# Attention and long convolution in one kernel: a filter reversal placed later, a later last transpose, more blocks for VectorE near the end, four extra matmuls

## The chip, the cores and the metric

The kernel runs on one core of a Trainium2 chip. The metric is the device time in microseconds (us) of one execution. Executions of the kernel before took 864.25, 865.54, 867.79 and 869.4 us; their median is 866.66 us.

The core has a matrix engine (TensorE, PE in the profile; PEld are its weight loads), a vector engine (VectorE, DVE), a scalar engine (ScalarE, ACT), GpSimd (POOL) and SyncE (SP). Here POOL and SP mostly issue transfers. Matrix products land in PSUM[...].

## The reference: two halves side by side

With S = 2048 positions and D = 512 channels, the left half of the output is multi-head attention with 32 heads of 16 channels:

```
qkv = x @ wqkv;  p = softmax(q k^T * 16**-0.5);  left = (p v) @ wo
```

The right half is a gated long convolution, written with FFTs in the reference:

```
k_shift = causal 4-tap convolution of k with shift_k
kv      = k_shift * v
y       = causal convolution of kv with ssm_k (2048 taps per channel) + kv * ssm_D
right   = q * y
```

## The kernel before: blocks, steps and two planned orders

**Attention.** Scores are made in blocks of 128 keys x 512 queries for one head. There are 2048 such blocks: 4 query blocks x 8 groups of 4 heads x 16 key tiles x 4 heads. They are handled in 741 steps, numbered by `T`. In a step TensorE writes two or three blocks into two or three PSUM banks (`emit_qk`, line 536), and ScalarE turns them into exponentials with one instruction (`PT`, line 547). Even and odd steps use different banks (0 to 2 and 3 to 5). Two steps later TensorE multiplies the exponentials by the values (`pv_step`, `emit_pv`, line 629). When all blocks of a group of heads are in, VectorE transposes, divides and transposes back (`finish_group`, lines 693 to 715), and the output projection uses the result (`op_mm`, line 746).

The number of blocks of a step is fixed in `banks_of`: 2 in odd steps below 184 and in 75 steps that leave a bank to other work, 2 as soon as at most `2 * N_TAIL` blocks are left, else 3. With `N_TAIL = 9` the last eight steps (733 to 740) have two blocks each.

**Exponentials on VectorE.** In some steps of three blocks, VectorE takes the exponential of the third block in five passes of 128 x 512 (`exp_on_dve`, lines 583, 590 three times, 595). `dve_block` decides in which. It refuses steps below 56 and from `NT - N_TAIL - GAP` = 741 - 9 - 7 = 725 on, and it refuses when the planned work of VectorE is too far ahead (`BACKLOG`). In the trace 212 blocks are made so, the last in step 724.

**Convolution.** The filter is reversed along its length, padded and stored to a scratch tensor in DRAM, so that each channel's Toeplitz matrix can be read with one transfer of overlapping rows. VectorE makes the reversal: four copies of 128 x 2048 (`kz_turn`, line 423) that wait for `h_kzl`, the last of three loads on one semaphore (two of the filter, one of `ssm_D`), then `kz_store` (line 428) adds `ssm_D` and issues the store. `kz_turn` also issues, after its second copy, the transposed load of the first half of k (`load_kt(0)`), and `kz_store` issues that of the second half; both go to the SP queue, and a small POOL memset goes with each. All later Toeplitz loads (512 of 512 KB, line 784 by way of 220) are on the SP queue too, and wait for the store.

The convolution itself is 128 quads of four channels (`conv_lags`, line 801, bank `BGB` = 7). After eight quads, `conv_turn` (line 827) transposes the sums, which VectorE has copied from PSUM into `YB` (line 816), and VectorE multiplies them by q into `QN` (line 836). The last `conv_turn` is issued from `emit_bg` itself, and when nothing is left for bank 7, `emit_bg` issues `keep_busy` (line 1012), a matmul whose result nobody reads, once a step until step 731. Others of that kind are made by `warm_up` (line 1007) where a gap is planned. From step 732 on, `tail_mm` makes the first three quarters of the projections of the last query block.

**What sets the order.** A planner in the kernel's code writes each engine's instruction list before the program is built. Each engine has a planned clock (`pe.t`, `dve.t`) and each instruction a planned duration. VectorE's work that isn't urgent lies in lists (`flow`); `pick` takes the entry that can start earliest and whose `gate()` is true, and `urgent` and `advance` let such entries in before the next urgent instruction. On the chip each engine runs its list in that order, and waits on semaphores.

At the very end, outside the loop, `op_mm(qb, 3, 0, 3, ...)` makes the first three quarters of the fourth projection tile, and then each of four tiles gets its last quarter as soon as its part of the last transposed group (`OTN`) is there; VectorE and ScalarE copy the results out in turn (`op_out_end`, lines 764 and 766), and four transfers store them.

## Time and profile before

| what | before |
|---|---|
| median of 4 executions | 866.66 us |
| the profiled execution, its own time | 865.5 us |
| its span in the profile | 863.8 us |
| ScalarE busy | 838.1 us, 97% |
| VectorE busy | 780.3 us, 90% |
| TensorE busy | 741.7 us, 86% |
| first exponential starts | 9.35 us |
| last exponential ends | 856.2 us |
| steps, blocks on VectorE | 741, 212 |

The span runs from the first to the last instruction that the profiler saw. An engine's row gives its busy time; the rest of the span it waited or had nothing to do. "Idle before" a row is that engine's wait just ahead of it, and the name behind the arrow is what ended the wait. PEclk is the share of its clock that TensorE was granted. In the list by time, a row with x3 merges three instructions in a row.

### The profile page before, as it was taken

To read this page: it belongs to the slowest core of one execution; us is meant where nothing else is said; L and a number is where in the kernel's file an instruction comes from. 1 tells how busy PE (TensorE), PEld (TensorE's weight loads), DVE (VectorE), ACT (ScalarE), POOL (GpSimd) and SP (SyncE) were. 2 spreads that over 40 slices of the span, in tenths; PEclk is the share of its full clock that TensorE was granted. 3 is DMA by queue.
4 is the path that set the end of the run, shared out by engine and by line. 5 is a ranking of instruction groups with operands and counts; after the bars stand their busy time and mean duration, and the time that the engine had idled before them with its cause. 6 is when DMAs were issued, how large, how long until landed. Compare 5 with 4: busy or idle time off the path is not lost.

```text
span 863.8 us, 29370 instructions
## 1 busy us (share of the span) xinstructions
PE 741.7 (86%) x13142; PEld 302.9 (35%) x13180; DVE 780.3 (90%) x1325; ACT 838.1 (97%) x746; POOL 17.4 (2%) x33
## 2 busy tenths in 40 slices
PE   7888999998888888888888888888888889888877
PEld 2223343443333333333333333334333333333332
DVE  3228899999999999999999999999999999999992
ACT  6999999999999999999999999999999999999996
POOL 2000000000000000000000010000000000000000
PEclk9999899999999999999999999999999999999998
DMA  9960069779999999999999999999999999999941
GB/s 270 267 225 1 1 194 338 249 257 319 407 408 408 385 395 395 405 407 404 380 397 380 359 407 391 387 363 379 407 409 378 377 399 410 408 406 407 408 157 57
DMA packets 104813, 289.36 MB, mean 335 GB/s; under 512 B 35184, under 2 KB 37232, under 8 KB 104304
## 3 DMA queue, kind: packets, MB, share of 16 engines
q1 hardware_dynamic: 99424, 279.35, 85.8%
q0 software_dynamic: 1808, 6.29, 2.1%
q8 instruction: 104, 1.70, 0.8%
q10 hardware_dynamic: 3456, 1.84, 0.8%
q14 instruction: 21, 0.17, 0.0%
HBM read 276.83 MB, written 6.42 MB: 328 GB/s over the span
## 4 chain that ended last, share of the span: by engine, by line
ACT 53%; DVE 20%; DMA 13%; PE 9%; SPq 2%; issue 2%; ACTq 0%
ACT PT L547 53%; DMA WR<-kz_scratch 12%; DVE EH L590 9%; PE PS L536 3%; DVE FX L583 3%; DVE PTD L595 3%; SPq L220 2%; PE PS L629 2%; PE PS L801 2%; DMA WR<-in_B_ssm_D_dram 1%; DVE QT L377 1%; DVE DT L693 1%; DVE YB L816 1%; PE PS L746 0%; DVE QN L836 0%
## 5 line engine op out<-in xcount | busy, mean ns | idle before, releaser
L547 ACT ACTIVATE PT<-PS 128x1536 bf16<-128x1536 f32 (+1 forms) x741 | 835.1, 1345 | 12.5 <-PE PS L536 11.3
L536 PE MATMUL PS<-QT,KTo 32*128 32x512 bf16 x2048 | 304.7, 389 | 86.5 <-ACT PT L547 68.5
L590 DVE SCALAR_TENSOR_TENSOR EH<-EH,FX 128x512 f32<-128x512 f32 x424 | 281.2, 679 | 0.1
L801 PE MATMUL PS<-WR,KV 128*5 128x128 bf16 (+15 forms) x8192 | 223.3, 221 | 13.5 <-DMA WR<-kz_scratch 11.5
L629 PE MATMUL PS<-PT,VAF 128*32 128x512 bf16 x1836 | 202.7, 394 | 5.0 <-DVE DT L693 3.4
L801 PEld LDWEIGHTS PS<-WR,KV 128*2 128x2 bf16 (+15 forms) x8192 | 149.2, 88 | 99.2 <-issue 40.0
L536 PEld LDWEIGHTS PS<-QT,KTo 32*128 32x128 bf16 x2048 | 73.0, 91 | 264.3 <-ACT PT L547 225.5
L583 DVE TENSOR_SCALAR FX<-PS 128x512 f32<-128x512 f32 x212 | 144.8, 683 | 7.5 <-PE PS L536 7.1
L595 DVE SCALAR_TENSOR_TENSOR PTD<-EH,FX 128x512 uint16<-128x512 f32 x212 | 143.2, 677 | 0.3 <-PE PS L629 0.3
L590 DVE SCALAR_TENSOR_TENSOR EH<-FX 128x512 f32<-128x512 uint16 x212 | 142.8, 682 | 0.0
L629 PEld LDWEIGHTS PS<-PT,VAF 128*32 128x32 bf16 x1836 | 48.6, 93 | 120.8 <-issue 106.2
L1007 PE MATMUL PS<-IDN,ZW 128*32 128x512 bf16 (+3 forms) x228 | 72.2, 317 | 0.3 <-PE PS L629 0.3
L629 PE MATMUL PS<-PTD,VAF 128*32 128x512 bf16 x212 | 60.8, 388 | 0.0
L693 DVE STREAM_TRANSPOSE DT<-PS 128x512 f32<-128x512 f32 x31 | 22.1, 712 | 16.9 <-PE PS L629 16.5
L402 DVE CAST VAF<-PS 128x512 bf16<-128x512 f32 x16 | 11.1, 691 | 27.9 <-PE PS L360 27.9
L1007 PEld LDWEIGHTS PS<-IDN,ZW 128*32 128x32 bf16 x228 | 22.0, 96 | 11.6 <-issue 10.3
L377 DVE TENSOR_SCALAR QT<-PS,MASK 128x512 bf16<-128x512 f32 x30 | 21.0, 742 | 3.0 <-PE PS L332 2.8
L816 DVE CAST YB<-PS 128x512 bf16<-128x512 f32 x32 | 21.8, 681 | 1.1 <-PE PS L801 0.9
L360 PE MATMUL PS<-WKV,xT 128*128 128x512 bf16 x59 | 17.7, 383 | 3.7 <-DVE VAF L402 2.6
L746 PE MATMUL PS<-WKV,OTN 128*128 128x512 bf16 x53 | 18.6, 411 | 2.2 <-issue 1.0
L341 PE MATMUL PS<-xT,WKV 128*128 128x512 bf16 (+1 forms) x57 | 16.7, 376 | 2.0 <-issue 1.0
L382 DVE CAST KTo<-PS 128x512 bf16<-128x512 f32 (+1 forms) x16 | 10.7, 670 | 7.7 <-PE PS L341 7.6
(64 smaller groups left out, 202.6 us busy)
## 6 DMA issues: line engine op xcount, KB each, us to landing
WR<-kz_scratch SPq DMA_DIRECT2D x512, 512.0 KB, 8.0
kz_scratch<-WR SPq DMA_DIRECT2D x1, 2176.0 KB, 8.6
QN<-in_B_q_dram POOLq DMA_DIRECT2D x2, 1024.0 KB, 12.4
out_dram<-QN POOLq DMA_DIRECT2D x2, 1024.0 KB, 8.2
out_dram<-OUTA POOLq DMA_DIRECT2D x12, 128.0 KB, 5.4
QN<-in_B_ssm_k_dram SPq DMA_DIRECT2D x1, 1024.0 KB, 5.9
QT<-in_B_ssm_k_dram SPq DMA_DIRECT2D x1, 1024.0 KB, 7.9
WR<-in_B_v_dram SPq DMA_DIRECT2D x2, 512.0 KB, 7.0
```

Source lines behind the costliest of these rows:

```text
L377: lambda e, par=par: e.tensor_scalar(QT[:, qb % 2, 2 * o + par, :], PS[:, bank, :], MASK[:, par:par + 1], None, ALU.mult),
L536: ins = e.matmul(PS[:, bank, :], lhsT=KTo[32 * s:32 * s + 32, g // 2, kt * 128:(kt + 1) * 128], rhs=QT[32 * s:32 * s + 32, qb % 2, g, :], ...
L547: h_exp[T] = act.op(lambda e: e.activation(PT[:, T % R_PT, 0:n * QB], PS[:, banks[0]:banks[0] + n, :].rearrange("p b f -> p (b f)"), ACT.E ...
L583: h_f = urgent(lambda e: e.tensor_scalar(fx, PS[:, bank, :], FIX_ADD, FIX_HI, ALU.add, ALU.min), [h, h_last.get(i - R_FX)], slack=0.6)
L590: st["h"] = dve.op(lambda e: e.scalar_tensor_tensor(eh, src, (A3, A2, A1)[j], frac, ALU.add, ALU.mult), [st["h"], h_last.get(i - R_EH), h_ ...
L595: lambda e: e.scalar_tensor_tensor(out16, eh, A4, fx, ALU.mult, ALU.add),
L629: ins = e.matmul(dst, lhsT=w, rhs=rhs, start=(k == 0), stop=(k == KT - 1), tile_position=(0, 32 * s))
L693: h_t = urgent(lambda e: e.transpose(out=dt, in_=PS[:, pvb(n), :]), [h] + before, slack=0.1, us=(0.63, 0.751))
L746: ins = e.matmul(PS[:, bank, :], lhsT=OTN[:, (4 * qb + o) % R_O, t * 128:(t + 1) * 128], rhs=WO[:, o, :], start=(o == 0), stop=(o == 3))
L801: ins = e.matmul(PS[32 * c:32 * c + NB - n, BGB, 128 * (kk % 4):128 * (kk % 4) + 128], lhsT=KV[:, qd, n:NB, c], rhs=WR[:, r + c, 128 * (NB ...
L816: hh = urgent(lambda e: e.tensor_copy(YB[:, half, :].rearrange("p (k i) -> p k i", k=4), src), [h, h_yb[0]], slack=0.3, us=V512)
L1007: pe.op(lambda e: e.matmul(PS[32 * s:32 * s + 32, pvb(n), 0:128 * k], lhsT=ZW[:, :], rhs=rhs, start=False, stop=False, tile_position=(0, 3 ...
```

## The change

Five constants and four places are touched.

- `N_TAIL` goes from 9 to 7: the steps of two blocks at the end begin at step 734. There are six of them, and the last step (740) has one block. The number of steps stays 741, since 184 + 75 + 475 steps come before.
- `dve_block` uses a new constant `TAIL_GAP = 4` in place of `GAP = 7`: its bound goes from step 725 to 741 - 7 - 4 = 730.
- The four reversals get a gate: the planner lets one in only when VectorE's planned clock is at least 4 us (`KZ_LATE`) past the planned landing of `h_kzl`.
- The last `conv_turn` is put off, step by step, while the planned end of VectorE's copy into `YB` isn't at least 0.2 us before TensorE's planned clock; at the latest it is issued in step 731.
- At the end, `KEEP` = 4 matmuls of 128 x 128 by 128 x 512 are added between the three quarters of the fourth projection tile and the four last quarters. They wait for the last exponential, and write the bank that it read; nobody reads their result.

```diff
-N_TAIL = 9
+N_TAIL = 7
...
 GAP = 7
+TAIL_GAP = 4
 AHEAD = 4
+KZ_LATE = 4.0
+KEEP = 4
...
     for c in (2, 3, 0, 1):
-        piece(lambda us, c=c: kz_turn(c, us), lambda: [h_kzl])
+        piece(lambda us, c=c: kz_turn(c, us), lambda: [h_kzl], gate=lambda: dve.t >= at(h_kzl) + KZ_LATE)
     piece(kz_store, lambda: [h_kzt[0]], (0.1, 0.22))
...
     def dve_block(T):
-        if len(banks_of[T]) < 3 or T < T_DVE or T >= NT - N_TAIL - GAP:
+        if len(banks_of[T]) < 3 or T < T_DVE or T >= NT - N_TAIL - TAIL_GAP:
             return None
...
         if st["turn"] and st["qd"] == C // 4:
+            if T < min(tail_mm) - 1 and at(h_ybw[0]) > pe.t - 0.2:
+                return
             conv_turn(C // 32 - 1, BGB)
...
     op_mm(qb, 3, 0, 3, tail_banks[3])
+    for i in range(KEEP):
+        pe.op(lambda e: e.matmul(PS[:, banks_of[NT - 1][0], :], lhsT=IDN[:, :], rhs=WO[:, 0, :], start=True, stop=True),
+              [h_exp[NT - 1]], inc=i == KEEP - 1)
     for t in range(4):
         h = op_mm(qb, t, 3, 4, tail_banks[t])
```

## Prediction

> **What bounds the kernel now.** I read the busy shares and slices of the page first.

> ```profile
> span 863.8 us, 29370 instructions
> PE 741.7 (86%) x13142; PEld 302.9 (35%) x13180; DVE 780.3 (90%) x1325; ACT 838.1 (97%) x746; POOL 17.4 (2%) x33
> ACT  6999999999999999999999999999999999999996
> ```

> ScalarE works from 9.35 to 856.2 us with hardly a pause, and those 847 us hold 741 exponentials and about 11.3 us of waits of over 0.08 us each (I summed the "idle before" of its rows in order of time). So only three things shorten the kernel: fewer blocks on ScalarE, shorter waits of ScalarE, or a shorter end after 856.2. The groups of instructions, shapes apart, give the price of a block:

> ```profile
> L547 ACT ACTIVATE PT<-PS 128x1536 bf16<-128x1536 f32 x354 | 528.5, 1559 | 8.5 <-PE PS L536 8.0
> L547 ACT ACTIVATE PT<-PS 128x1024 bf16<-128x1024 f32 x387 | 409.7, 1148 | 4.1 <-PE PS L536 3.3
> ```

> 528.5 / 354 = 1.493 and 409.7 / 387 = 1.059: a block is 0.43 us. Then the head, VectorE and SP by time:

> ```profile
> 15.04 0.42 DVE L382 CAST KTo<-PS 128x256 bf16<-128x256 f32 x1 [1.03 <-PE PS L341]
> 17.63 1.30 DVE L423 COPY WR<-QN 128x2048 bf16<-128x2048 bf16 x2 [2.17 <-DMA WR<-in_B_ssm_D_dram]
> 18.84 0.69 DVE L402 CAST VAF<-PS 128x512 bf16<-128x512 f32 x1
> 19.45 1.29 DVE L423 COPY WR<-QT 128x2048 bf16<-128x2048 bf16 x2
> ...
> 27.59 6.12 SPq L220 DMA_TRANSPOSE QN<-in_B_k_dram  x1
> 33.83 0.50 SPq L220 DMA_DIRECT2D kz_scratch<-WR  x1
> ```

> VectorE stood 2.17 us at the reversal before its transfer had landed, and a copy of values queued behind came at 18.84. SP took up the loads that need the reversal only at 27.59. What ScalarE lost there:

> ```profile
> 20.56 1.02 ACT L547 ACTIVATE PT<-PS 128x1024 bf16<-128x1024 f32 x1 [0.56 <-PE PS L536]
> ...
> 23.57 4.66 ACT L547 ACTIVATE PT<-PS 128x1024 bf16<-128x1024 f32 x4 [0.36 <-PE PS L536]
> ```

> Last the end: TensorE and ScalarE by time, and the granted clock in stretches (columns: length, busy time of PE, PEld, DVE, ACT, POOL, then clock, DMA share, GB/s).

> ```profile
> 837.40 0.62 PE L827 MATMUL PS<-IDN,YB 128*128 128x128 bf16 x8 [1.14 <-DVE YB L816]
> 838.39 2.79 ACT L547 ACTIVATE PT<-PS 128x1536 bf16<-128x1536 f32 x2 [0.31 <-PE PS L536]
> 843.40 12.81 ACT L547 ACTIVATE PT<-PS 128x1536 bf16<-128x1536 f32 x12 [0.59 <-PE PS L536]
> 858.79 1.89 PE L746 MATMUL PS<-WKV,OTN 128*128 128x512 bf16 x4 [0.52 <-DVE OTN L715]
> ...
> 835.80:839.20 3.40, 1.74 (x21) 0.92 (x22) 3.29 (x6) 3.09 (x4) 0.16 (x1) 1.00 0.00 0
> 839.20:842.60 3.40, 3.40 (x17) 0.62 (x17) 3.25 (x6) 3.22 (x3) 1.02 (x1) 0.50 0.51 147
> ...
> 852.90:856.30 3.40, 2.41 (x19) 0.68 (x18) 0.00 (x0) 3.32 (x4) 0.00 (x0) 1.00 0.00 0
> 856.30:863.80 7.50, 3.64 (x8) 0.86 (x9) 3.67 (x9) 1.19 (x2) 0.00 (x0) 0.50 0.21 70
> ```

> The last `conv_turn` held TensorE for 1.14 us; the stretch in which that fell has 1.74 us of PE, and the next runs at half clock, in which ScalarE waits 0.18 and 0.59 us more. From 856.3 the clock is half again, for all of the final products.

> [...] the half-clock stretches here last 3.4 us or a multiple, and the two at the end each follow a thin one (1.74 and 2.41 us of PE; stretches with 2.98 and 3.40 were followed by a full clock). [...] the last four products start at 858.79, 859.19, 859.62 and 860.04, so 0.42 us apart. [...]

> **The change part by part**, against the profiled execution (865.5 us, of which 863.8 is the span; the median is 1.2 higher).

> *Reversal later.* No instruction is added. The four copies (1.30 + 1.29 us) go some 4 us later. There VectorE idles 0.47, 1.13, 2.30, 1.13 and 1.26 us ahead of its rows from 21.4 to 30.0 us, and the planner puts single copies of 0.65 us into such gaps. The 2.17 us wait goes, for the load landed at 17.6. ScalarE gets back at most 0.56 + 0.17 (at 21.75) + 0.36 + 0.16 (at 28.38) = 1.25 us; at least nothing, if the copies then hold up other casts. I take 0.8: the 0.56 wholly and part of the rest. What moves with it: two transposed loads and the store on SP, two memsets on POOL. The reversal would end near 24 to 26 us; SP is busy with x and v until 27.59 and takes the store at 33.83, POOL has nothing until 132 us. So it costs nothing with 2 to 8 us of cover; and past it, k is first multiplied at 93.5 us and the first load from the scratch is issued at 44, so some 50 us more. VectorE's order in between is otherwise the same, and a planner that only compares its own clocks with each other, when all of them shift alike, decides the same afterwards. So steps 30 to 724 should keep their order.

> *Last turn later.* TensorE then issues the scores of step 726 and their products first, one step of 1.33 us; the copy to `YB` ended at 837.35, so its wait is nearly over by then. Behind the waiting turn stood the scores of 726, and ScalarE behind those: 0.31 us back. If the stretch then holds enough PE work, the half clock at 839 goes too: 0.18 + 0.59 us. What is late next: `keep_busy` in the following step waits for VectorE's product into `QN` (it waited about 0.4 us before), and the 1024 KB store of `QN` on POOL leaves 1.3 us later, with its 8.2 us hidden under the 25 us to the end. Range 0 to 1.1, taken 0.6.

> *More blocks on VectorE.* ScalarE's blocks fell to two in steps 713, 716, 718, 721 and 724: one VectorE block per 2.6 steps. Five more steps (725 to 729) give 2, at 0.43 us each: 0.85 us back; one to three are 0.4 to 1.3. Their 5 x 0.6 us each lie in VectorE's idle time from 843.5 to 856.9 (13.41 us ahead of the last transpose). The change's own words say "up to step 722", which its code doesn't (730 is the bound); were it so, one block fewer, 0.4 us lost.

> *Tail of two-block steps.* The blocks are the same and so is the number of exponentials, so ScalarE's total stays. After the last exponential one product follows instead of two: 0 to 0.2 us, taken 0.1.

> *Four matmuls at the end.* If the clock is half (as before), the three products start at 856.81 and take 3 x 0.43 to 858.1, the four new ones 1.7 more to 859.8, and the first final product starts there instead of at 858.79: 1.0 us lost. If it is full, all seven (1.5 us) end by 858.4, behind VectorE's 1.5 us of transpose, reciprocal and product, and cost nothing, and the four final ones, 0.22 apart, end about 0.8 us earlier. [...] I take 0.1 lost, with -0.9 and +1.0 as ends.

> Sum: -0.8 - 0.6 - 0.85 - 0.1 + 0.1 = -2.25 us: 863.2 of 865.5, and 864.4 at the median. About 0.5%, 4.3 us, is what a measurement of this kernel can tell from no change, so this is within it.

> **Rivals.**

> *A larger gain.* The reversal's wait depends on when a transfer lands; the median execution is 1.2 us longer than the profiled one, and if that lies there, the head is worth 1.25 + 1.2 = 2.4. With 0.9 for the turn and 1.3 for three blocks, that is 4.6: 862.0. [...] Against: every part must be at its good end.

> *Slower, by half-clock windows.* The order of the long middle stays but its phase against the windows moves. The middle has five such stretches (at 92, 566, 645, 675 and 764 us), with ScalarE waits of 1.37, 1.98, 0.92, 1.17 and 0.68: 1.2 us each. Two more cancel the gain; six more give -2.25 + 7.2 = +5 us, 871.6. [...] Against: shifts of a microsecond or two come between executions anyway, and those lie within 5 us.

> *Not what it says.* The last VectorE block stays at 722, and the four matmuls run cold: -0.8 - 0.6 + 0.4 + 1.0 = 0: 866.7.

> *A transfer that becomes the bound.* Loads of the Toeplitz rows run at about 400 GB/s from 220 us on; a later start would show at the end. It doesn't start later, by the cover above: the same 864.4.

> **How the numbers follow.** The forecast (with the hidden transfer) has 0.50, the larger gain 0.33, not what it says 0.09, slower 0.08. So faster by over 0.5%: 0.33, within: 0.59, slower: 0.08. The forecast's own range is 862.8 to 866.3. For 8 in 10 the range reaches down into the larger gain, to 860.8, and up past "not what it says", to 867.0.

> **What would show it.** The row of line 423 with no wait for the DMA and starting after 20 us; no ScalarE wait near 20.56; SP's store still at about 33.8. The last `conv_turn` one step later with a wait under 0.3 us. Some 214 blocks on VectorE, the last past step 724. ScalarE's last exponential 2 us earlier. The last four products 0.22 apart (full clock) or starting about 1 us later against the last transpose (half). I am wrong if the middle's order differs, or if SP's loads of k move past 27.6 us.

## Result, and the profile after

The median went from 865.88 us (63 executions, those beside it on the same chip among them) to 862.76 us (44 executions). The ratio is 0.9967, with a 95% interval from 0.9953 to 0.998: 0.33% faster, or 2.9 us (1.7 to 4.1). The ratio leaves out the few executions that were over 1.5% slower than the fastest of their kernel. That is a real gain, but within the 0.5% that the prediction set as its bound. The profiled execution took 863.4 us by its own time.

The page of the kernel after, span and busy shares:

```profile
span 861.7 us, 29386 instructions
PE 735.8 (85%) x13146; PEld 302.7 (35%) x13184; DVE 783.8 (91%) x1330; ACT 836.9 (97%) x746; POOL 17.4 (2%) x33
```

ScalarE still bounds the kernel. Instruction by instruction, all five engines have the same order as before except in three places: VectorE's first casts and the reversal, what TensorE, VectorE and ScalarE do from step 725 on, and the four added matmuls. TensorE's order in the head is unchanged. (In the middle only the interleaving of matmuls that run side by side differs here and there.)

The head after, VectorE, SP and ScalarE by time:

```profile
20.56 0.69 DVE L405 CAST VAF<-PS 128x512 bf16<-128x512 f32 x1 [1.89 <-PE PS L363]
21.17 1.28 DVE L426 COPY WR<-QN 128x2048 bf16<-128x2048 bf16 x2
22.39 0.69 DVE L385 CAST KTo<-PS 128x512 bf16<-128x512 f32 x1
22.99 1.28 DVE L426 COPY WR<-QT 128x2048 bf16<-128x2048 bf16 x2
...
27.88 6.25 SPq L223 DMA_TRANSPOSE QN<-in_B_k_dram  x1
34.24 0.51 SPq L223 DMA_DIRECT2D kz_scratch<-WR  x1
...
22.71 4.66 ACT L550 ACTIVATE PT<-PS 128x1024 bf16<-128x1024 f32 x4 [0.25 <-PE PS L539]
```

The reversal starts at 21.17 and waits for nothing. SP issues the loads of k and the store at the same place of its list, 0.3 to 0.4 us later than before (27.59 and 33.83): it was busy with the load of v ahead of them until 27.84, and the reversal had ended at 24.3. ScalarE's waits there fall from 1.25 to 0.41 us.

The end after, TensorE and ScalarE by time:

```profile
837.84 0.62 PE L830 MATMUL PS<-IDN,YB 128*128 128x128 bf16 x8
839.57 0.39 PE L1012 MATMUL PS<-IDN,ZW 128*32 128x512 bf16 x1 [0.64 <-DVE QN L839]
833.43 21.36 ACT L550 ACTIVATE PT<-PS 128x1536 bf16<-128x1536 f32 x19 [0.47 <-PE PS L539]
857.36 0.81 PE L749 MATMUL PS<-WKV,OTN 128*128 128x512 bf16 x3 [0.51 <-DVE OTN L718]
```

And one of its stretches with the granted clock (length, busy time of PE, PEld, DVE, ACT, POOL, clock, DMA share, GB/s):

```profile
837.40:840.80 3.40, 2.69 (x27) 1.13 (x25) 3.26 (x6) 3.40 (x3) 1.17 (x1) 1.00 0.00 0
```

The last turn waits for nothing now, TensorE is busy for 2.69 us of that stretch instead of 1.74, the clock stays full (1.00 in this stretch and in the next, 840.80 to 844.20), and ScalarE runs 19 exponentials from 833.43 to the last without a wait. The last three of the four final products take 0.81 us together, 0.22 from one to the next, at a granted clock of 1.00 (857.30 to 858.20); four took 1.89 before, at 0.50.

Where the two profiled executions differ, cut at the starts of ScalarE's exponentials of steps 0, 30 and 725 and at the end of the last one:

| stretch | before, us | after, us | difference |
|---|---|---|---|
| start to step 0 | 9.35 | 9.56 | +0.2 |
| steps 0 to 29 | 35.59 | 34.54 | -1.05 |
| steps 30 to 724 | 791.65 | 792.92 | +1.3 |
| steps 725 to 740 | 19.62 | 17.78 | -1.84 |
| after the last exponential | 7.54 | 6.88 | -0.66 |
| span | 863.76 | 861.67 | -2.1 |

The middle, whose instructions are the same, is the one that got longer; the experiments show how little that one number means.

### The profile page after: what moved, and what is told of

Its sections match the earlier page's. It is cut to its first block, busy times and chain, and to the rows that moved or that the text cites. A ratio compares the mean times of both kernels' runs of the same rounds, so it can differ in the third digit from the quotient of the medians.

```text
span 861.7 us, 29386 instructions
## 1 busy us (share of the span) xinstructions
PE 735.8 (85%) x13146; PEld 302.7 (35%) x13184; DVE 783.8 (91%) x1330; ACT 836.9 (97%) x746; POOL 17.4 (2%) x33
## 3 DMA queue, kind: packets, MB, share of 16 engines
q10 hardware_dynamic: 3456, 1.84, 0.8%
## 4 chain that ended last, share of the span: by engine, by line
ACT 65%; DMA 13%; DVE 9%; PE 9%; issue 2%; SPq 1%; ACTq 0%
ACT PT L550 65%; DMA WR<-kz_scratch 12%; DVE EH L593 4%; PE PS L539 3%; PE PS L804 2%; PE PS L632 2%; DVE FX L586 2%; SPq L223 1%; DVE PTD L598 1%; DMA xT<-in_A_x_dram 1%; PE PS L363 1%; PE PS L749 0%; DVE VAF L405 0%; DVE QT L380 0%; DVE DT L696 0%
## 5 line engine op out<-in xcount | busy, mean ns | idle before, releaser
L550 ACT ACTIVATE PT<-PS 128x1536 bf16<-128x1536 f32 (+1 forms) x741 | 833.9, 1345 | 12.1 <-PE PS L539 11.1
L539 PE MATMUL PS<-QT,KTo 32*128 32x512 bf16 x2048 | 302.9, 386 | 86.0 <-ACT PT L550 69.7
L335 PE MATMUL PS<-xT,WQ 128*128 128x512 bf16 x46 | 15.0, 383 | 2.4 <-issue 1.4
```

The source lines that it names most:

```text
L539: ins = e.matmul(PS[:, bank, :], lhsT=KTo[32 * s:32 * s + 32, g // 2, kt * 128:(kt + 1) * 128], rhs=QT[32 * s:32 * s + 32, qb % 2, g, :], ...
L550: h_exp[T] = act.op(lambda e: e.activation(PT[:, T % R_PT, 0:n * QB], PS[:, banks[0]:banks[0] + n, :].rearrange("p b f -> p (b f)"), ACT.E ...
```

## Experiments: what each part is worth, and a half clock in the head

Each kernel was timed beside the kernel before. The stretches are those of one profile of each run; the ratio is that of its timed executions:

| run | steps 0 to 29 | 30 to 724 | 725 to 740 | after | ratio to before (95%) |
|---|---|---|---|---|---|
| before | 35.59 | 791.65 | 19.62 | 7.54 | |
| gate alone | 34.52 | 792.88 | 19.55 | 7.32 | 0.9991 (0.9959 to 1.0023) |
| turn alone | 39.75 | 793.33 | 18.42 | 6.89 | 0.999 (0.9959 to 1.0021) |
| N_TAIL, TAIL_GAP alone | 38.03 | 786.84 | 20.39 | 6.86 | 0.9979 (0.9956 to 1.0003) |
| four matmuls alone | 38.21 | 789.73 | 19.60 | 8.00 | 0.9996 (0.9969 to 1.0023) |
| after | 34.54 | 792.92 | 17.78 | 6.88 | 0.9967 (0.9953 to 0.998) |
| after, gate undone | 35.81 | 792.30 | 17.93 | 6.88 | 0.9988 (0.9965 to 1.001) |
| before with a filler | 35.86 | 788.17 | 20.74 | 6.89 | 0.9979 (0.9959 to 0.9999) |
| after, reversal 20 us late | 34.53 | 791.39 | 17.93 | 6.87 | 0.9976 (0.9955 to 0.9998) |
| after, one more block | 34.53 | 794.28 | 17.55 | 6.88 | 0.997 (0.9946 to 0.9993) |
| after, more fillers | 34.54 | 790.98 | 17.85 | 6.88 | 0.9975 (0.9956 to 0.9994) |
| after, four matmuls undone | 34.53 | 790.27 | 17.94 | 6.88 | 0.9939 (0.9908 to 0.997) |
| after, delay in the head | 46.53 | 785.99 | 17.85 | 6.87 | 1.0087 (1.0059 to 1.0115) |

The expectations weigh several readings. The sum theory is the prediction's own sum. The head theory puts nearly all of the gain into steps 0 to 29, the end theory puts it after step 724. The clock theory came up after the first four runs: the stall of TensorE in the head can bring on a half clock (under the tail alone: 2.08 us of PE in a stretch of 3.40, then 0.50 in the next two). Such a stretch, cut where the profile shows the half clock begin or end, is called a window below.

**The gate alone (e1_gate_only).** Edit, against the kernel before:

```diff
-        piece(lambda us, c=c: kz_turn(c, us), lambda: [h_kzl])
+        piece(lambda us, c=c: kz_turn(c, us), lambda: [h_kzl], gate=lambda: dve.t >= at(h_kzl) + KZ_LATE)
```

> Only the gate on the reversals. Sum theory: 0.8 us faster than before (0 to 1.25); VectorE's reversal row has no DMA wait and starts after 20 us, ScalarE's waits from 9 to 30 us fall from 1.25 to about 0.4 us, SP's store stays near 34 us. Head theory (nearly all of the gain lies in the head): 2.4 to 3 us faster. End theory (the gain lies after step 724): 0.

Measured: 864.26 us beside 865.88. ScalarE's waits fell to 0.41 us and the reversal started at 21.22, as expected; the store left at 34.7. Its time alone can't be told from no change.

**The turn alone (e2_turn_only).**

```diff
         if st["turn"] and st["qd"] == C // 4:
+            if T < min(tail_mm) - 1 and at(h_ybw[0]) > pe.t - 0.2:
+                return
             conv_turn(C // 32 - 1, BGB)
```

> Only the last turn put off. Sum theory: 0.6 us faster (0 to 1.1), the turn one step later with a wait under 0.3 us, and no 0.31 us wait of ScalarE at step 726. Head theory: 0. End theory: 1 us or more. The reversal's wait for its transfer is as in the kernel before, near 2.2 us if the landing is steady, and anything from 0 to 4 us if it isn't.

Measured: 863.95 us. From step 725 to the last exponential it took 18.42 us instead of 19.5 to 19.6 (before, gate alone, four matmuls alone), so the turn is worth about 1.15 us, just past the upper end of its range (0 to 1.1). The half clock behind the turn is what goes. The three profiles just named have it at 837.9 to 839.9, and the two remaining ones with the old turn go to half clock for 6.8 us from 836.0 and 833.7. None of the eight profiles with the new turn has a half clock between step 725 and the last exponential.

But the head of this run was not that of the kernel before. VectorE waited for the same landing, at 17.69, and ScalarE lost 5 us in steps 0 to 29.

**The tail alone (e3_tail_only).**

```diff
-N_TAIL = 9
+N_TAIL = 7
+TAIL_GAP = 4
-        if len(banks_of[T]) < 3 or T < T_DVE or T >= NT - N_TAIL - GAP:
+        if len(banks_of[T]) < 3 or T < T_DVE or T >= NT - N_TAIL - TAIL_GAP:
```

> Only N_TAIL = 7 and TAIL_GAP = 4. One more block on VectorE (213): sum theory 0.43 for the block and 0.1 for the shorter last step, 0.5 us faster. Head theory: 0. End theory: 1 us or more.

Measured: 863.83 us, 213 blocks. One more block is 0.43 us less for ScalarE, but its end is hidden in this profile by the half clock of the old turn (2.11 us of waits after step 724). With the new turn the block shows: 18.42 without it, 17.78 to 17.94 with it (after and four others).

The head of this run shows what happened in three of the five profiles with an ungated reversal and no filler. VectorE, TensorE and ScalarE by time:

```profile
17.94 1.29 DVE L424 COPY WR<-QN 128x2048 bf16<-128x2048 bf16 x2 [2.35 <-DMA WR<-in_B_ssm_D_dram]
19.89 0.77 PE L361 MATMUL PS<-WKV,xT 128*128 128x512 bf16 x2 [1.26 <-DVE VAF L403]
21.24 1.02 ACT L548 ACTIVATE PT<-PS 128x1024 bf16<-128x1024 f32 x1 [1.13 <-PE PS L537]
23.30 1.45 ACT L548 ACTIVATE PT<-PS 128x1536 bf16<-128x1536 f32 x1 [1.04 <-PE PS L537]
25.97 4.80 ACT L548 ACTIVATE PT<-PS 128x1024 bf16<-128x1024 f32 x4 [1.22 <-PE PS L537]
```

The stretches of the same run with their clock (columns as above):

```profile
16.80:20.20 3.40, 2.08 (x14) 0.52 (x13) 2.26 (x4) 3.31 (x3) 0.12 (x1) 1.00 1.07 222
20.20:23.60 3.40, 3.16 (x14) 0.55 (x13) 1.70 (x4) 1.32 (x2) 0.12 (x1) 0.50 1.19 241
23.60:27.00 3.40, 3.40 (x17) 0.70 (x16) 0.69 (x1) 2.17 (x2) 0.00 (x0) 0.50 0.98 195
```

And the stretches of the kernel before that answer to the first two:

```profile
16.60:20.00 3.40, 2.27 (x14) 0.52 (x13) 2.37 (x4) 3.40 (x3) 0.12 (x1) 1.00 1.11 226
20.00:23.40 3.40, 2.94 (x18) 0.81 (x17) 1.76 (x5) 2.48 (x2) 0.12 (x1) 1.00 1.08 235
```

The wait has the same cause in all six profiles with the old reversal, but not the same length: 2.17 us before, 2.35 here, 2.54 and 2.75 in the two other runs that lost the clock (four matmuls alone, turn alone). It holds the cast behind it, so TensorE stands for 1.1 to 1.7 us. In the profile of the kernel before, the window around it had 2.27 us of PE and the clock stayed; here it had 2.08 and the clock was half for 6.8 us, around which ScalarE lost three times over 1 us. In those two others the window had 1.90 and 1.74. So in these four profiles, where one window holds the whole stall, its PE time falls as the wait grows. In the profile after, the windows of this place have 2.90 us and more, and none of the six gated profiles without an added delay has a half clock in the head.

**The four matmuls alone (e4_keep_only).**

```diff
     op_mm(qb, 3, 0, 3, tail_banks[3])
+    for i in range(KEEP):
+        pe.op(lambda e: e.matmul(PS[:, banks_of[NT - 1][0], :], lhsT=IDN[:, :], rhs=WO[:, 0, :], start=True, stop=True),
+              [h_exp[NT - 1]], inc=i == KEEP - 1)
```

> Only the four added matmuls. Sum theory: between 1.0 us slower (half clock at the end: the first final product starts about 1 us later against the last transposes) and 0.9 faster (full clock: the final products 0.22 apart), near 0 on the mean. End theory: 1 us faster.

Measured: 866.11 us. The end, TensorE and VectorE by time:

```profile
858.88 1.78 PE L1042 MATMUL PS<-WKV,IDN 128*128 128x512 bf16 x4
859.24 0.89 DVE L716 STREAM_TRANSPOSE OTN<-DTN 128x128 bf16<-128x128 bf16 x4
860.49 1.03 PE L747 MATMUL PS<-WKV,OTN 128*128 128x512 bf16 x4
```

The four take 1.78 us at half clock, 0.43 from one to the next (the final products of the kernel before, at 0.50, started 0.42 apart; the four take 1.03 in the profile after, at 1.00 from 855.80 to 857.00). The first final product starts 1.25 us after the last group's transposes begin; before it was 0.37 (858.79, from here):

```profile
858.42 0.89 DVE L715 STREAM_TRANSPOSE OTN<-DTN 128x128 bf16<-128x128 bf16 x4
```

That is 0.9 us lost; 0.4 came back, since the clock was full again for the final four (1.03 us), and the end took 8.00 us against 7.54. Where the clock is full it takes 6.86 to 6.89 us with them or without.

**The gate undone (e5_gate_undone)**, the changed kernel with the reversal's line as before:

```diff
-        piece(lambda us, c=c: kz_turn(c, us), lambda: [h_kzl], gate=lambda: dve.t >= at(h_kzl) + KZ_LATE)
+        piece(lambda us, c=c: kz_turn(c, us), lambda: [h_kzl])
```

> The changed kernel without the gate: the reversal where it was. Clock theory (TensorE's stall behind the waiting reversal makes a window thin, and the next one or two run at half clock, in most executions): ScalarE waits 3 to 4 us from 9 to 32 us, a half-clock stretch that begins between 20 and 22 us, and about 2.5 us slower than the changed kernel. Sum theory of the prediction: 1.25 us of waits, no half clock there, 0.8 us slower.

Measured: 865.17 us, 0.9988 against 0.9967 with the gate, so the gate is worth 0.2% or 1.8 us here, with an error of some 2.3 us. Its profile has the wait (2.38 us) but no half clock, as the kernel before had it: a miss for the expectation of the clock theory in this profile. The wait is as long as in the tail alone (2.35), which lost its clock; but here a boundary of the windows, at 19.5, cuts the stall of 18.95 to 20.24 in two:

```profile
16.10:19.50 3.40, 2.79 (x20) 0.67 (x20) 1.21 (x2) 3.40 (x4) 0.00 (x0) 1.00 1.06 290
19.50:22.90 3.40, 2.20 (x14) 0.60 (x15) 2.75 (x6) 2.45 (x3) 0.25 (x2) 1.00 0.99 214
```

**A filler in the stall (e6_filler)**, the kernel before with four matmuls of zeros at step 8:

```diff
         pv_step(T)
+        if T == 8:
+            for i in range(4):
+                pe.op(lambda e: e.matmul(PS[0:32, pvb(0), :], lhsT=ZW[:, :], rhs=bass.AP(
...
+                    start=False, stop=False, tile_position=(0, 0)), [h_zw, h_idn], us=(0.0, 0.0))
```

> The kernel before with four more matmuls of zeros (128 x 32 by 128 x 512, 0.9 us of TensorE) put into TensorE's stall at step 8, planned at no time so that all else keeps its order. Clock theory: VectorE still waits about 2.2 us for the transfer, but there is no half-clock stretch near 20 us, and ScalarE's waits from 9 to 32 us are about 1.3 us instead of 3.4; about 2 us faster than the kernel before. If the wait itself cost the 3.4 us: no change.

Measured: 864.11 us, a ratio of 0.9979 (0.9959 to 0.9999). VectorE still waited 2.43 us, there was no half clock, TensorE had 2.92 us of work in the window around the stall, and ScalarE's waits were 1.51 us. The executions were 1.8 us (0.1 to 3.6) faster without the wait being touched. The one profile doesn't prove the mechanism, since two without a filler had no half clock either; the time points the same way, at the edge of what it can tell.

**The reversal much later (e7_late20)**

```diff
-KZ_LATE = 4.0
+KZ_LATE = 20.0
```

> The changed kernel with the reversal 20 us past the planned landing instead of 4. SP's loads of k and the store then wait for VectorE and are issued some 10 us later (near 38 and 44 us). Sum theory: the cover of 50 us hides all of it, time as the changed kernel. The rival of a transfer that becomes the bound: 10 us slower.

Measured: 863.14 us. VectorE and SP by time:

```profile
36.80 1.28 DVE L426 COPY WR<-QN 128x2048 bf16<-128x2048 bf16 x2
...
38.12 4.06 SPq L223 DMA_TRANSPOSE QN<-in_B_k_dram  x1
42.30 0.51 SPq L223 DMA_DIRECT2D kz_scratch<-WR  x1
```

SP was held by the reversal for 10 us and the first Toeplitz load left at 52.5 instead of 44.4, and nothing came of it: the head took 34.53 us. The cover is there, and the rival of a transfer that becomes the bound is out for delays up to that size.

**One more block, no added matmuls (e8_more_blocks)**

```diff
-TAIL_GAP = 4
-KEEP = 4
+TAIL_GAP = 1
+KEEP = 0
```

> The changed kernel with TAIL_GAP = 1 and without the four matmuls at the end. VectorE takes one more block (214, the last in step 730): 0.43 us less on ScalarE. The end after the last exponential: 6.9 us at full clock, 7.4 at half clock (the four matmuls made it 8.0 at half clock and didn't shorten it at full). Together 0.4 to 0.9 us faster than the changed kernel.

Measured: 864.15 us, ratio 0.997: no difference from the changed kernel that can be seen. 214 blocks, and 17.55 us from step 725 on, 0.2 to 0.4 less than with 213; it drowns in the middle, which took 794.28 in that profile.

**More fillers (e9_more_fillers)**, on top of the last one:

```diff
-BUSY = 0.75
-FILL_GAP = 0.25
+BUSY = 0.9
+FILL_GAP = 0.1
```

> The kernel with one more VectorE block and without the four matmuls at the end (TAIL_GAP = 1, KEEP = 0), and the planner lets a filler matmul into gaps of TensorE from 0.1 us on (0.25 before) up to 0.9 of a window (0.75 before); 329 planned fillers instead of 232, so the order of the middle changes too. Clock theory: fewer half-clock stretches between 30 and 800 us than the 3 to 6 of the other runs, each worth about 1.1 us of ScalarE, so 1 to 3 us faster than the changed kernel. Rival: the fillers stand in front of the scores in TensorE's queue and cost what they save; no change or slower.

Measured: 863.9 us, 0.9975. VectorE took 215 blocks here, one more than in the last run. One half-clock stretch was left between 30 and 800 us. That count tells less than the expectation meant, since four of the other runs (tail alone, filler, four matmuls undone, delay in the head) have one too. But in those ScalarE waited 4.9, 6.6, 8.3 and 5.3 us in the middle, and in this one 9.9, and it is no faster than the changed kernel. So the rival's number holds, but its cause isn't shown: only 0.7 us of those 9.9 come right behind a filler. The two longest, 2.34 and 1.36 us, stand behind a late Toeplitz load and behind a `conv_turn` that waited for VectorE. TensorE and ScalarE at the first:

```profile
496.06 0.41 PE L804 MATMUL PS<-WR,KV 128*16 128x128 bf16 x16 [2.72 <-DMA WR<-kz_scratch]
496.84 4.63 ACT L550 ACTIVATE PT<-PS 128x1024 bf16<-128x1024 f32 x4 [2.34 <-PE PS L539]
```

**The four matmuls undone (e10_keep_undone)**

```diff
-KEEP = 4
+KEEP = 0
```

> The changed kernel without the four matmuls at the end. From the last exponential to the end 6.9 us if the clock is full to the last product (as with them), 7.3 to 7.5 if it goes half before (with them 8.0 in the run that had them alone). End theory (they keep the clock up): 0.5 us or more slower than the changed kernel. Sum theory: within 0.3 us of it.

Measured: 861.11 us, 0.9939 (0.9908 to 0.997). The end took 6.88 us, as with them:

```profile
854.83 1.04 PE L749 MATMUL PS<-WKV,OTN 128*128 128x512 bf16 x4 [1.15 <-DVE OTN L718]
```

It beats the kernel before; its interval overlaps that of the changed kernel, and its profile has no line that the missing matmuls would explain, so no more is claimed than that nothing shows a use of them. One case stays open: in the run of the gate alone the clock fell 1.8 us after the last exponential, between it and the final products, and the end took 7.32 us. No profile with the four has a window that ends there, so whether they would have saved that one isn't known.

**A delay in the head (e11_head_delay)**, the changed kernel with 56 of the zero matmuls at step 8:

```diff
         pv_step(T)
+        if T == 8:
+            for i in range(56):
+                pe.op(lambda e: e.matmul(PS[0:32, pvb(0), :], lhsT=ZW[:, :], rhs=bass.AP(
...
+                    start=False, stop=False, tile_position=(0, 0)), [h_zw, h_idn], us=(0.0, 0.0))
```

> The changed kernel with 56 matmuls of zeros (12.1 us of TensorE at full clock) put in at step 8, planned at no time so that every other instruction keeps its place. It prices a microsecond lost in the head. If it goes through to the end: 11 to 12 us slower than the changed kernel (ScalarE has less than 1 us of work ahead there). If the middle, where TensorE waits for Toeplitz loads, takes part of it back (the waits of TensorE for those loads, 11 to 18 us in the runs so far, would fall): 9 us slower or less. In the second case the gate's gain of about 3 us in the head would be worth about 2 at the end.

Measured: 872.89 us, 1.0087 (1.0059 to 1.0115). The head grew by 12.0 us (46.53 against 34.54). Against the changed kernel's 0.9967 the time grew by 1.2%, 10.4 us (7.7 to 13.1). So most of a microsecond lost in the head is lost at the end. Whether all of it is, this doesn't settle: TensorE's waits for Toeplitz loads were 12.2 us, at the low end of the 11.5 to 18.5 of the others, and the middle of this profile took 785.99 us.

## Why the prediction was right, and where a term was mis-sized

The forecast was 864.4 us and within 0.5%; 862.76 came, at a slightly faster median of the kernel before. In microseconds gained: 2.25 forecast, 2.9 (1.7 to 4.1) measured. That the sum came so close is in part luck: the head's term was too small, the one for the blocks too large, and the parts as the profiles show them add up to more than was measured. By its steps:

- **The middle keeps its order.** Right, on every engine.
- **Reversal later, 0.8 us.** The mechanism is right, and against the profiled execution so was the size (1.25 to 0.41 us of waits). The term is mis-sized over several profiles: the one it was read from happened to keep its clock. Steps 0 to 29 took 35.59, 35.81, 38.03, 38.21 and 39.75 us with the old reversal and no filler, 37.5 on the mean, and 34.5 with the gate in all six profiles without an added delay: 3 us instead of 0.8. The rival of a larger gain had nearly that size (2.4), with half of the cause. It blamed a landing that varies; from its issue the load of `ssm_D` took 7.6 us to land in the profiles before and after alike. The reversal could start at 17.54 to 18.29 in all six profiles with the old reversal, and VectorE's wait for it was 2.17 to 2.75 us. But those 0.6 us alone aren't the loss: they help to decide how much work TensorE has in the window around its stall (2.27 us of PE before, and the clock stayed; 2.08, 1.90 and 1.74 in the three runs that lost it), which that rival didn't name. The place of the window is the other half. The prediction cut the end of the kernel into such stretches, and not the head. With nearly the same wait (2.35 and 2.38 us), the stall of the tail alone lies in one window (2.08 us of PE, then a clock of 0.50), that of the gate undone in two (2.79 and 2.20, at 1.00 in both).
- **SP and POOL past the reversal: nothing.** Right; shown with a delay of 10 us. One of the prediction's own signs of being wrong was met by the letter, since the loads of k left at 27.88, past 27.6; but what held them was the load of v ahead of them, not the reversal.
- **Last turn, 0.6 of at most 1.1.** Just past the upper end: about 1.15. The half clock behind it went. What was said to be late next was: `keep_busy` waited 0.64 us for `QN`, and ScalarE didn't notice.
- **Two more blocks, 0.85.** One, 0.43: the last VectorE block is in step 728, not 722 as the change's own words have it. I took the spacing of 2.6 steps from the steps before; from 724 on it was 4 to the next. That `YB`'s copy and `QN`'s product, which fall there, leave less room is what the lists suggest; it wasn't tested.
- **Tail and four matmuls, 0.** The cost at half clock, which the prediction also calls cold, is as worked out for the first final product (0.9 of 1.0 us), 0.46 of it at the end. The gain at full clock needs no added matmuls: the end is 6.9 us wherever the clock is full to the last product, and it was so in all six profiles with the new end that were not delayed, with and without them.

What stays open: the parts add up to more than was measured. The head's 3.0 (against a mean of five profiles that range over 4 us), 1.75 from step 725 on (19.6 to 17.85, against the three profiles with one half-clock stretch there) and 0.2 in the end are 4.9 us. With the head of two of the five profiles, which kept their clock (35.6 and 35.8, so 1.2 us), they would be 3.1. So either the timed executions have the half clock in the head less often than three times in five, which no view of them shows, or the middle takes something back. The timed executions put the gate at 0.8 us (alone) and 1.8 (undone), each with an error of more than 2, so they show neither the 3.0 nor that it is less. For the second reading the delay of 12 us leaves room, but the profiles speak little for it. The middle varies from 786.0 to 794.3 us, and much of that goes with one stall near 565 us (last section): with it, it is 791.8 on the mean of four ungated profiles and 792.3 of five gated ones; the four profiles without it have 786.0 to 791.0.

## What to carry to other kernels

A wait of about 2 us on one engine can cost more than itself where it leaves TensorE idle. In the tail alone VectorE's wait of 2.35 us left TensorE 2.08 us of work in a window of 3.4, the clock was half for the next 6.8, and steps 0 to 29 took 38.03 us instead of 34.5. So ask of each stall not only what is queued behind it, but whether it makes a window of TensorE thin. A single profile shows one place of that window: its bounds around the same stall were 16.6 and 20.0 us before, 16.8 and 20.2 in the tail alone, 16.1 and 19.5 in the gate undone. Look at the same place in several executions before its price is taken from one. Work that waits for a transfer, with other work behind it in its engine's list (here a cast behind a wait of 2.17 us), is best put where the transfer has surely landed, as long as a view shows what covers the delay (the reversal at 36.80 instead of 21.17 left the head at 34.53 us).

## What the runs showed of the hardware that I had not expected

```profile
88.30:91.70 3.40, 2.56 (x19) 0.70 (x18) 3.35 (x7) 3.40 (x4) 0.00 (x0) 1.00 0.00 0
272.60:276.00 3.40, 1.96 (x62) 0.97 (x62) 3.04 (x6) 3.40 (x3) 0.00 (x0) 1.00 1.02 407
```

- Near 565 us TensorE stands ahead of one and the same weight load, the 8,508th instruction of its list in the trace, in nine of the thirteen profiles: 1.1 to 2.7 us with no wait that the profile shows, and each time the clock is half afterwards. In the other four it doesn't. Three of those four are the runs with more matmuls ahead of that place in TensorE's list (filler, more fillers, delay); the fourth, the tail alone, has the same list up to there as the kernel before. Whether the place in the list matters wasn't tested. The middle of the nine takes 789.7 to 794.3 us, of the four 786.0 to 791.0. From the kernel after:

```profile
563.70 0.39 PE L804 MATMUL PS<-WR,KV 128*15 128x128 bf16 x15
566.75 0.27 PE L804 MATMUL PS<-WR,KV 128*12 128x128 bf16 x5 [2.66 <-issue]
```

Its cause is open. The two means differ by 4.1 us (792.1 and 788.0), more than any part of this change and than the whole of it; how much of that is the stall's own, and not the other differences of those four kernels, isn't shown.
